# Another fixed order for chunks 0 to 5 of a chunked recurrence and for the weight conversion beside it, and a ring of five tiles

## The chip, the cores and the metric

One Trainium2 chip, one core. The metric is the device time of one execution in microseconds (us), the median of three runs.

## What is computed

A recurrence over 768 steps for 4 x 8 heads of 40 x 40 state, and two layers on its output. Cut to the core of the reference:

```python
for t in range(S):                       # S = 768, B = 4, H = 8, D = 40
    y[:, :, t] = einsum('bhd,bhde->bhe', r_t, state)
    Sa = einsum('bhde,bhe->bhd', state, a_t)
    state = state * w_t - einsum('bhd,bhe->bhde', Sa, b_t) + einsum('bhd,bhe->bhde', v_t, k_t)
x = y as 3072 rows of 320
g = elu(x @ w_in); x = g @ w_out         # first MoE: 320 -> 2048 -> 320
P = exp(x @ w_gate - max), 8 rounds of row and column scaling
out = sum over 8 experts of P[:, e] * (relu(x @ w1[e]) @ w2[e])   # 320 -> 1024 -> 320
```

The weights of the first MoE come as 64-bit floats, read as pairs of 32-bit words.

## The kernel before

**The recurrence** is cut into 24 chunks of 32 steps. For a chunk, products over all pairs of its steps are made with matmuls, a triangular system is solved, and the state goes on to the next chunk. The work of a chunk is split into functions, named by what they do:

- `loadw`, `loadk`, `loadv`, `loads2` (tokens `ldw`, `ldk`, `lu`, `lv`) issue the loads of the chunk's inputs on SyncE's DMA queue: tiles `WA`, `KE`, `VU`, `rB` and `rO`.
- `prep` (lines 331 to 355) has five steps: the scan of decays into `F` on VectorE, reciprocal and second scan into `xE`, a product `aE`, copies on ScalarE, and two products that write `KE` in place (line 355, on VectorE in chunks 0 and 1, on GpSimd later).
- `E3` (masked products, line 383, evicted by VectorE into `Am`) writes the chunk's matrix to DRAM (`Ad`, line 400); `LT` reads it back, spread over the partitions (line 408). `E1` transposes `KE` into `KB`, `E2` (line 369) transposes `xE` into `xT`.
- `tsolve` (token `u` with two chunks, then `s_n` for n steps) solves the systems of two chunks together on VectorE, two short instructions a step (lines 436 and 438, tiles `Tt` and `Wk`). The result goes to DRAM and back on SyncE's queue (`Td`, line 460, `TT`, line 464).
- `H1` to `H4` carry the state: `H1` makes the right-hand side `RH`, `H2` multiplies by the solved matrix (line 510) and corrects the second half of the chunk (lines 500 and 501), `H3` makes the new state `Y` (line 534), `YW` scales it on GpSimd (line 486). `O1`, `O2`, `O3a`, `O3b` make the output: `O1` copies into `uE` on ScalarE and VectorE, `O2` a masked product `Gm`, `O3b` multiplies by `xT` and writes the rows to DRAM (`yd`).

**The conversion** of the first MoE's weights is 32 pieces, 16 of `w_in` (384 wide) and 16 of `w_out` (320 wide). Token `d` loads a piece into `raw` (two buffers for each size), `b` puts the words together in three VectorE instructions (lines 214 to 216, tile `tmp`), `o` rounds and takes the remainder on ScalarE and GpSimd into `Wt` and `Wo` (lines 238 to 245).

**The first MoE** runs beside the recurrence in units of 128 hidden columns (token `m`): eight matmuls into `ph` (line 638), the activation on ScalarE and VectorE (`m`, `g`, line 647; `gh`, `gl`, line 651 on GpSimd), and, two units later, eight matmuls into two accumulators (lines 665 to 669). Token `x` transposes the next block of rows. A unit can only run when its weights are converted.

**The order** of all this is written by hand, as tokens. The table `START` covers chunks 0 to 3 whole, the early steps of chunks 4 to 7 and the whole conversion. After it a loop over chunks runs the table `order2` for chunks 4 and 5 and `order` for the rest; `+3` in a token is a chunk ahead, `p` three steps of a running solve. The instructions of TensorE, VectorE, ScalarE and GpSimd are pinned to that order, queue by queue. SyncE's queue is not: a scheduler places its DMAs.

```python
for t in tokens(PLAN["start"]):
    ...
    pin_since(last, late_queue=PLAN["queue"])   # "queue": False
```

After the last chunk the rest of the first MoE and the second MoE follow, with TensorE busy throughout.

Of the kernel before, what the change touches and what calls it, by code (L numbers as in the profile page):

```python
# [9 lines left out]
F32 = mybir.dt.float32  # L10
# [10 lines left out]


START = """
lu_0 prep_0*5 E3_0 ldw_2 E3_0 LT_0 E1_0 E2_0 prep_1*5 E3_1*2 LT_1 ldk_2 E4_0 H1_0 E1_1 E2_1 lu_1 d*2 lv_0 b o u_0_1 d b o prep_2 d prep_2*2 ldw_3 b
s_10 s_11 b prep_2 s_10 o d prep_2 E3_2 b o E3_2 LT_2 E2_2 ldk_3 H2_0 o E1_2 prep_3*2 d*2 H2_0 prep_3 H2_0 O1_0 H3_0 prep_3*2 E3_3 b H3_0 o O1_0 d
E3_3 YW_1 ldw_4 b E4_1 LT_3 O2_0 H1_1 E1_3 prep_4 ldk_4 E2_3 u_2_3 b o d O2_0 s_10 O3b_0 d lu_2 o H2_1 O3a_0 O3b_0 s_10 H2_1 s_10 prep_4 H2_1 prep_4
ldw_5 H3_1*2 b o d O1_1*2 H4_1 lv_1 YW_2 O2_1 E4_2 prep_4*2 E3_4 b O3a_1 d O2_1 o prep_5 H1_2 O3b_1 b E3_4 LT_4 o O3b_1 s_9 E1_4 ldk_5 xl E2_4 d
prep_5 H2_2 prep_5 x*2 b x*2 H2_2 prep_5 m prep_5 o ldw_6 b o d m H2_2 d E3_5 b m E2_5 E3_5 H3_2*2 E1_5 ldk_6 o d O1_2 prep_6*2 lu_3 m O1_2 H4_2 YW_3
E4_3 m b o d u_4_5 prep_6 H1_3 lv_2 b O2_2 ldw_7 m o O2_2 d LT_5 H2_3 b o d s_10 m H2_3 O3a_2 b o d m O3b_2*2 H2_3 prep_6*2 b prep_7 ldw_8 d o H3_3 m
E3_6 H3_3 b o d m E3_6 E2_6 E1_6 ldk_7 m b d o LT_6 s_10 prep_7 O1_3 H4_3 lu_4 b YW_4 m d o O1_3 b o lv_3 O2_3 b o d m O2_3 prep_7 b o d m O3a_3 b  # L30
O3b_3 s_20 d b o m d m prep_7 b m o prep_7 m*2 O3b_3 d m o d m x b o b d m x b d o*2 x*2 b o
"""


# [5 lines left out]
    "start": START,  # L40
    "tp": ((3, 3), (3, 3)),
    "queue": False,
# [71 lines left out]
def build(ctx, tc, r, k, v, w, a, b, w_in, w_out, wg, w1, w2, wa_d, kb_d, re_d, ro_d, vt_d, wp_d, consts, out, C, off):  # L114
# [13 lines left out]
    V, A, G, T, SY = nc.vector, nc.scalar, nc.gpsimd, nc.tensor, nc.sync  # L128
# [49 lines left out]
    r2 = rec.enter_context(tc.tile_pool(name="r2", bufs=2, side="right"))  # L178
# [178 lines left out]
    def unpad(dst, ps):  # L357
        return dst.rearrange("p (j g e) -> p j g e", j=2, g=NG), ps.rearrange("p (g x) -> p g x", g=NG)[:, :, 0:128].rearrange("p g (j x) -> p j g x", j=2)[:, :, :, 0:D]
# [9 lines left out]

    def E2(c):
        z = st[c]  # L370
        z.xT = r2.tile([128, 384], F32, tag="xT", name="xT", bufs=4)
        xv = z.xC
        for g in range(NG):
            T.transpose(PS["E2"][0][:, 128 * g:128 * g + HR], xv[0:HR, g, :], ident[0:HR, 0:HR])
        o, i = unpad(z.xT[:, 0:DM], PS["E2"][0])
        cp("XT", 0, o, i)
# [91 lines left out]
    def cp(n, i, out, in_):  # L468
        (A.copy if PLAN["eng"][n][i] == "A" else G.tensor_copy if PLAN["eng"][n][i] == "G" else V.tensor_copy)(out=out, in_=in_)
# [661 lines left out]
    with ExitStack():  # L1131
# [37 lines left out]
        mg = msteps()  # L1169
        wgen = [(k, i) for i in range(NF1) for k in "io"]  # L1170
        fns = dict(ld=loads, ldw=loadw, ldk=loadk, lu=loadv, lv=loads2, prep=prep, H1=H1, H2=H2, H3=H3, H4=H4, E1=E1, E2=E2, E3=E3, E4=E4, T=tsolve, O1=O1, O2=O2, O3a=O3a, O3b=O3b, YW=YW, LT=LT)
        done = {("ld", 0), ("ld", 1)}

# [140 lines left out]
```

## Time and profile before

| | us |
|---|---|
| median of three runs | 2249.49 |
| lowest and highest run | 2245.49 and 2250.47 |
| the profiled execution | 2250.63 |
| its span, first to last instruction | 2248.8 |

The profile shows for every engine (PE is TensorE, DVE VectorE, ACT ScalarE, POOL GpSimd, SP SyncE) when it was busy, and what ended its idle time. A line of the timeline has the start, the duration and, in brackets, the idle time in front and its releaser. The granted clock is that of TensorE: 1.00 is its level of 2.4 GHz, 0.50 that of 1.2 GHz.

### The profile page before, as it was taken

Reading aid. Unit: us, or ns where it says so; the run is one execution under the profiler, and the core shown is the slowest. Engines: PE = TensorE matmul, PEld = TensorE weight load, DVE = VectorE, ACT = ScalarE, POOL = GpSimd, SP = SyncE. Lnnn points to the kernel's source line nnn. Section 1 sums busy time; section 2 is a strip of 40 time slices with the busy share of each in tenths; the row PEclk is TensorE's granted clock in tenths of the full one; section 3 lists DMA queues with packets and bytes.
Section 4 is the critical chain, followed back from the end, with each engine's and each line's share of the span. In section 5 each row is a group of like instructions: output and inputs, shape, how many; then the busy total and the mean of one; then the engine's idle time right before and its main releaser. Section 6 shows DMA issues by size and latency. Waiting matters only on the chain.

```text
span 2248.8 us, 48229 instructions
## 1 busy us (share of the span) xinstructions
PE 2137.9 (95%) x20483; PEld 1934.8 (86%) x20483; DVE 928.5 (41%) x1889; ACT 815.0 (36%) x1813; POOL 439.7 (20%) x545
## 2 busy tenths in 40 slices
PE   3788999999999999999999999999999999999998
PEld 2677888999898989898888888888888888888888
DVE  6686667777766322532222222222222222222222
ACT  2344555555544565223224324223224212112111
POOL 2354333443433261002002002002002002001000
PEclk9676999999999999999999999999999999999999
DMA  6654434344442142002113112002002001000000
GB/s 161 165 161 107 114 102 100 95 110 111 105 105 72 45 122 56 29 1 56 20 20 75 23 32 78 26 27 78 27 26 65 1 1 52 1 1 20 24 24 25
DMA packets 216657, 138.50 MB, mean 62 GB/s; under 512 B 143793, under 2 KB 192306, under 8 KB 216434
## 3 DMA queue, kind: packets, MB, share of 16 engines
q1 hardware_dynamic: 216434, 135.34, 22.9%
q8 instruction: 162, 2.65, 0.5%
q14 instruction: 61, 0.50, 0.1%
HBM read 116.80 MB, written 18.48 MB: 60 GB/s over the span
## 4 chain that ended last, share of the span: by engine, by line
PE 79%; DVE 9%; DMA 4%; issue 2%; ACT 2%; SPq 2%; POOL 1%; DVEq 0%; ACTq 0%; POOLq 0%
PE h L874 28%; PE pa L918 10%; PE pa L919 10%; PE pa L917 10%; PE ph L638 5%; PE h L863 2%; PE a L665 2%; DVE Wk L452 2%; DVE Tt L445 2%; DMA yd<-xT 1%; PE P L534 1%; PE a L666 1%; PE a L667 1%; PE P L383 1%; PE P L510 1%
## 5 line engine op out<-in xcount | busy, mean ns | idle before, releaser
L878 DVE SCALAR_TENSOR_TENSOR hl<-h,hh 128x512 fp32r<-128x512 f32 x384 | 265.3, 691 | 765.9 <-ACT hh L877 765.4
L877 ACT ACTIVATE hh<-h 128x512 fp32r<-128x512 f32 x384 | 229.6, 598 | 899.2 <-PE h L874 897.5
L874 PE MATMUL h<-xs,a 128*128 128x512 f32 x2280 | 547.0, 394 | 0.2 <-DVE hl L878 0.2
L874 PEld LDWEIGHTS h<-xs,a 128*128 128x128 f32 x2280 | 421.0, 188 | 109.8 <-issue 25.4
L918 PE MATMUL pa<-a,hl 128*128 128x320 f32 x1536 | 475.8, 310 | 0.8 <-DVE hl L878 0.8
L919 PE MATMUL pa<-a,hh 128*128 128x320 f32 x1536 | 475.2, 309 | 0.0
L917 PE MATMUL pa<-a,hh 128*128 128x320 f32 x1536 | 473.9, 309 | 0.3 <-ACT logits L692 0.3
L918 PEld LDWEIGHTS pa<-a,hl 128*128 128x128 f32 x1536 | 288.9, 188 | 6.7 <-DVE hl L878 1.7
L917 PEld LDWEIGHTS pa<-a,hh 128*128 128x128 f32 x1536 | 288.6, 188 | 5.2 <-ACT logits L692 0.4
L919 PEld LDWEIGHTS pa<-a,hh 128*128 128x128 f32 x1536 | 289.0, 188 | 0.0
L825 POOL TENSOR_TENSOR a<-rw,a 128x384 fp32r<-128x384 f32 x64 | 65.2, 1019 | 1057.5 <-ACT a L823 1044.4
L638 PE MATMUL ph<-X,Wt 128*128 128x256 f32 x1536 | 234.8, 299 | 8.2 <-DVE g L647 7.8
L651 POOL TENSOR_TENSOR gl<-g,gh 128x256 fp32r<-128x256 f32 x192 | 150.1, 782 | 385.1 <-ACT gh L649 305.0
L638 PEld LDWEIGHTS ph<-X,Wt 128*128 128x128 f32 x1536 | 212.2, 205 | 13.1 <-DVE g L647 11.5
L647 DVE SCALAR_TENSOR_TENSOR g<-m,ph 128x256 f32<-128x256 f32 x192 | 79.9, 416 | 205.0 <-ACT m L641 147.9
L928 DVE SCALAR_TENSOR_TENSOR acc<-pa,Pg,acc 128x320 f32<-128x320 f32 x168 | 81.0, 544 | 184.1 <-PE pa L919 184.1
L649 ACT ACTIVATE gh<-g 128x256 fp32r<-128x256 f32 x192 | 80.1, 417 | 163.5 <-DVE g L647 162.7
L452 DVE TENSOR_TENSOR Wk<-Wk,Tt 128x132 f32<-128x132 f32 (+24 forms) x279 | 109.4, 392 | 8.6
L874 PE MATMUL h<-X,a 128*128 128x512 f32 x456 | 108.9, 394 | 0.0
L640 ACT ACTIVATE m<-ph 128x256 f32<-128x256 f32 x192 | 73.0, 380 | 89.5 <-PE ph L638 86.4
L874 PEld LDWEIGHTS h<-X,a 128*128 128x128 f32 x456 | 84.1, 188 | 21.9 <-issue 5.0
L445 DVE TENSOR_TENSOR Tt<-Wk,LT 128x132 f32<-128x132 f32 (+24 forms) x279 | 90.1, 323 | 8.0
(189 smaller groups left out, 2700.3 us busy)
## 6 DMA issues: line engine op xcount, KB each, us to landing
LT<-Ad SPq DMA_DIRECT2D x22, 512.0 KB
rw<-in_moe_w SPq DMA_DIRECT2D x64, 160.0 KB
WA<-in_wa SPq DMA_DIRECT2D x23, 422.9 KB
KE<-in_kb SPq DMA_DIRECT2D x23, 416.0 KB
rw<-in_moe_w SPq DMA_DIRECT2D x64, 128.0 KB
VU<-in_vt SPq DMA_DIRECT2D x24, 320.0 KB
raw<-in_wp SPq DMA_DIRECT2D x16, 384.0 KB
rchk<-in_wp SPq DMA_DIRECT2D x16, 384.0 KB
```

What stands on the lines that cost most here:

```text
L445: V.tensor_tensor(out=tv, in0=Wk[:, :, 0:ni, j:j + 1].to_broadcast(sh), in1=LT2[:, :, j, j + 1:C].unsqueeze(2).to_broadcast(sh), op=ALU.mult,)
L452: V.tensor_tensor(out=Wk[:, :, 0:ni, j + 1:C], in0=Wk[:, :, 0:ni, j + 1:C], in1=tv, op=ALU.subtract)
L638: T.matmul(ph, lhsT=Wt[0:kp, wi, 128 * f:128 * f + 128], rhs=X[0:kp, xi, :], start=(i == 0), stop=(i == 7))
L649: A.activation(out=gh, in_=g, func=AF.Copy)
L651: G.tensor_tensor(out=gl, in0=g, in1=gh.bitcast(F32), op=ALU.subtract)
L874: T.matmul(h, lhsT=a1[:, wi, :], rhs=X[bk][:, xi, :], start=(i == 0 and n == 8), stop=(i == n - 1), skip_group_check=(n == 7))
L877: dve["hh"] = A.activation(out=hh, in_=h, func=AF.Relu)
L878: V.scalar_tensor_tensor(out=hl, in0=h, scalar=0.0, in1=hh.bitcast(F32), op0=ALU.max, op1=ALU.subtract)
L917: T.matmul(o, lhsT=hh[:, ts_], rhs=a2[:, 0, :], start=(f == 0), stop=False)
L918: T.matmul(o, lhsT=hl[:, ts_], rhs=a2[:, 0, :], start=False, stop=False)
L919: T.matmul(o, lhsT=hh[:, ts_], rhs=a2[:, 1, :], start=False, stop=(f == NF2 - 1))
L928: V.scalar_tensor_tensor(out=at, in0=o, scalar=Pg[:, tt, e:e + 1], in1=at, op0=ALU.mult, op1=ALU.add)
```

## The change

It replaces the table `START` and the table `order2` by others with the same tokens (300 and 68 of them, each as often as before), and gives `xT` five tiles where it had four. The number of instructions on each engine stays. Two lines of the tables as an example, and the one line of code outside them:

```diff
-lu_0 prep_0*5 E3_0 ldw_2 E3_0 LT_0 E1_0 E2_0 prep_1*5 E3_1*2 LT_1 ldk_2 E4_0 H1_0 E1_1 E2_1 lu_1 d*2 lv_0 b o u_0_1 d b o prep_2 d prep_2*2 ldw_3 b
+prep_0*3 lu_0 prep_0*2 E3_0 ldw_2 E3_0 E2_0 prep_1*5 E3_1*2 LT_1 ldk_2 E1_1 E2_1 E4_0 H1_0 lu_1 d*2 lv_0 b o E1_0 u_0_1 d b o prep_2 d prep_2 LT_0
...
-        z.xT = r2.tile([128, 384], F32, tag="xT", name="xT", bufs=4)
+        z.xT = r2.tile([128, 384], F32, tag="xT", name="xT", bufs=5)
```

In `order2` the tokens `O3a`, `m`, `G`, `YW`, `O2` and one `E3` stand elsewhere.

**VectorE, the solve of chunks 0 and 1.** `Tt` and `Wk` are the solve's own tiles, `tmp` is a converted piece.

```order
 L436 TENSOR_TENSOR Tt<-Wk,LT 128x60
-L214 TENSOR_SCALAR tmp<-raw 128x320
-L215 SCALAR_TENSOR_TENSOR tmp<-raw,tmp 128x320
-L216 SCALAR_TENSOR_TENSOR tmp<-raw,tmp 128x320
 L438 TENSOR_TENSOR Wk<-Wk,Tt 128x4x3x5
...
 L436 TENSOR_TENSOR Tt<-Wk,LT 128x16
 L438 TENSOR_TENSOR Wk<-Wk,Tt 128x4x4
+L214 TENSOR_SCALAR tmp<-raw 128x320
+L215 SCALAR_TENSOR_TENSOR tmp<-raw,tmp 128x320
+L216 SCALAR_TENSOR_TENSOR tmp<-raw,tmp 128x320
 L214 TENSOR_SCALAR tmp<-raw 128x384
```

A piece of `w_out` (320 wide) that stood between two steps of the solve now stands behind its last step.

**SyncE's queue in the first microseconds.** `Ad` is the matrix of a chunk on its way to DRAM, `LT` the way back, `KE` the input of chunk 2, `raw` a piece to be converted.

```order
 L1242 DMA wgs<-in_moe_w_gate 64x8 x2
 L400 DMA Ad<-Am_114 32x8x32 x4
-L315 DMA KE<-in_kb 104x1024
 L327 DMA rO<-in_ro 104x512
...
 L226 DMA raw<-in_moe_w_out 128x640
-L226 DMA raw<-in_wp 128x768
-L310 DMA WA<-in_wa 104x1041
-L226 DMA raw<-in_moe_w_out 128x640
+L315 DMA KE<-in_kb 104x1024
+L226 DMA raw<-in_wp 128x768
+L310 DMA WA<-in_wa 104x1041
```

The load of `KE` for chunk 2 was behind the writes of chunk 0's matrix, ahead of both `LT` reads; it now stands behind both and behind a `raw` load. (`ldk_2` kept its place in the table; the buffer it writes is read by `E1_0`, which comes later now.)

**VectorE before the end of the solve of chunks 4 and 5.** `g` is a unit of the first MoE, `uE` the copy of `O1_3`, `F` the first scan of chunk 7.

```order
 L438 TENSOR_TENSOR Wk<-Wk,Tt 128x4x3x6
+L647 SCALAR_TENSOR_TENSOR g<-m,ph 128x256
 L336 SCALAR_TENSOR_TENSOR F<-WA,dr 104x528
 L214 TENSOR_SCALAR tmp<-raw 128x320
 L215 SCALAR_TENSOR_TENSOR tmp<-raw,tmp 128x320
 L216 SCALAR_TENSOR_TENSOR tmp<-raw,tmp 128x320
-L647 SCALAR_TENSOR_TENSOR g<-m,ph 128x256
-L469 COPY uE<-P_102 80x512
 L214 TENSOR_SCALAR tmp<-raw 128x384
 L215 SCALAR_TENSOR_TENSOR tmp<-raw,tmp 128x384
 L216 SCALAR_TENSOR_TENSOR tmp<-raw,tmp 128x384
+L469 COPY uE<-P_102 80x512
```

`g` goes ahead of the scan and of a piece, and `uE` goes behind the next piece.

## Rows read from the trace of the kernel before

**Rows 1.** The head of the page, and its row of the granted TensorE clock, 40 slices
```profile
span 2248.8 us, 48229 instructions
...
PEclk9676999999999999999999999999999999999999
```

**Rows 2.** Busy time by stretch: us, busy us of each engine, granted clock, DMA share, GB/s
```profile
core 0: us, PE busy (x) PEld busy (x) DVE busy (x) ACT busy (x) POOL busy (x), PEclk, DMA share, GB/s
...
111.00:177.00 66.00, 56.96 (x955) 51.92 (x955) 57.84 (x106) 29.46 (x71) 36.87 (x48) 0.71 0.57 163
177.00:198.00 21.00, 12.20 (x144) 11.00 (x144) 11.87 (x23) 8.56 (x22) 11.58 (x18) 0.75 0.49 126
198.00:218.00 20.00, 19.47 (x272) 18.07 (x272) 9.16 (x14) 8.85 (x22) 5.82 (x8) 0.50 0.25 68
218.00:258.00 40.00, 38.83 (x755) 36.69 (x754) 35.65 (x84) 22.08 (x56) 13.31 (x17) 1.00 0.37 96
...
900.00:2249.00 1349.00, 1341.86 (x7512) 1185.93 (x7510) 370.01 (x644) 368.81 (x706) 99.40 (x106) 1.00 0.11 30
```

**Rows 3.** TensorE's waits from 30 to 130 us: total, times, longest
```profile
PE P L510 <- DMA TT<-Td: 11.9, 2, 11.3
```

**Rows 4.** TensorE's waits from 130 to 210 us
```profile
PE P L383 <- DVE uE L469: 3.7, 1, 3.7
PE P L510 <- ACT RH L469: 3.6, 1, 3.6
PE ph L638 <- DVE g L647: 3.4, 2, 2.4
PE a L666 <- POOL gl L651: 3.1, 1, 3.1
```

**Rows 5.** Pieces of the chain that ended last: start, us, what
```profile
26.48 2.45 DMA Ad<-Am
29.08 3.69 DMA LT<-Ad
...
68.56 3.61 DMA Ad<-Am
...
178.22 1.95 DMA Td<-Wk
```

**Rows 6.** VectorE in order of time, around the first solve
```profile
32.86 0.22 DVE L436 TENSOR_TENSOR Tt<-Wk,LT 128x60 f32<-128x60 f32 x1 [0.45 <-DMA LT<-Ad]
...
40.84 0.32 DVE L214 TENSOR_SCALAR tmp<-raw 128x320 int32<-128x320 int32 x1
...
42.13 0.21 DVE L438 TENSOR_TENSOR Wk<-Wk,Tt 128x60 f32<-128x60 f32 x1
```

**Rows 7.** VectorE in order of time, around the second solve
```profile
76.11 0.22 DVE L436 TENSOR_TENSOR Tt<-Wk,two 128x60 f32<-128x60 f32 x1 [5.08 <-DMA two<-Ad]
...
84.30 1.25 DVE L336 TENSOR_TENSOR_SCAN F<-WA,dr 104x528 f32<-104x528 f32 x1
...
87.73 0.49 DVE L542 TENSOR_TENSOR Y<-P,Yw 104x320 f32<-104x320 f32 x1 [0.21 <-PE P L534]
88.14 0.46 DVE L214 TENSOR_SCALAR tmp<-raw 128x384 int32<-128x384 int32 x1
```

**Rows 8.** VectorE in order of time, around the third solve
```profile
163.69 0.33 DVE L214 TENSOR_SCALAR tmp<-raw 128x320 int32<-128x320 int32 x1 [0.63 <-POOL WoB L245]
...
170.59 0.41 DVE L647 SCALAR_TENSOR_TENSOR g<-m,ph 128x256 f32<-128x256 f32 x1
...
187.07 0.90 DVE L214 TENSOR_SCALAR tmp<-raw 128x384 int32<-128x384 int32 x1 [3.85 <-DMA raw<-in_wp]
```

**Rows 9.** The DMA queue of SyncE, the load of chunk 2
```profile
21.55 0.33 SPq L315 DMA_DIRECT2D KE<-in_kb  x1
```

**Rows 10.** TensorE, the same eight products at either clock
```profile
199.94 2.07 PE L638 MATMUL ph<-X,Wt 128*128 128x256 f32 x8
...
219.97 1.19 PE L638 MATMUL ph<-X,Wt 128*128 128x256 f32 x8
```

More of the change, by code (lines that the diff above doesn't have):

```diff
@@ L23 @@
 START = """
-lu_0 prep_0*5 E3_0 ldw_2 E3_0 LT_0 E1_0 E2_0 prep_1*5 E3_1*2 LT_1 ldk_2 E4_0 H1_0 E1_1 E2_1 lu_1 d*2 lv_0 b o u_0_1 d b o prep_2 d prep_2*2 ldw_3 b
-s_10 s_11 b prep_2 s_10 o d prep_2 E3_2 b o E3_2 LT_2 E2_2 ldk_3 H2_0 o E1_2 prep_3*2 d*2 H2_0 prep_3 H2_0 O1_0 H3_0 prep_3*2 E3_3 b H3_0 o O1_0 d
-E3_3 YW_1 ldw_4 b E4_1 LT_3 O2_0 H1_1 E1_3 prep_4 ldk_4 E2_3 u_2_3 b o d O2_0 s_10 O3b_0 d lu_2 o H2_1 O3a_0 O3b_0 s_10 H2_1 s_10 prep_4 H2_1 prep_4
+prep_0*3 lu_0 prep_0*2 E3_0 ldw_2 E3_0 E2_0 prep_1*5 E3_1*2 LT_1 ldk_2 E1_1 E2_1 E4_0 H1_0 lu_1 d*2 lv_0 b o E1_0 u_0_1 d b o prep_2 d prep_2 LT_0
+prep_2 ldw_3 b d prep_2 s_11 s_10*2 o b prep_2 E3_2 b o E3_2 o LT_2 E2_2 ldk_3 H2_0 E1_2 prep_3*2 d*2 prep_3 H2_0*2 O1_0*2 H3_0 prep_3*2 E3_3 b H3_0 o
+d E3_3 YW_1 ldw_4 b E4_1 LT_3 O2_0 H1_1 prep_4 E1_3 prep_4 ldk_4 E2_3 u_2_3 b o d O2_0 s_10 lu_2 o H2_1 d O3a_0 O3b_0*2 s_10 H2_1 s_10 H2_1 prep_4
 ldw_5 H3_1*2 b o d O1_1*2 H4_1 lv_1 YW_2 O2_1 E4_2 prep_4*2 E3_4 b O3a_1 d O2_1 o prep_5 H1_2 O3b_1 b E3_4 LT_4 o O3b_1 s_9 E1_4 ldk_5 xl E2_4 d
[L28 to L31, printed above, removed]
+prep_5 H2_2 x prep_5 x*2 b x H2_2 prep_5 m prep_5 o ldw_6 b o d H2_2 d E3_5 E2_5 m E3_5 b m H3_2*2 E1_5 ldk_6 o d O1_2 prep_6*2 lu_3 m O1_2 H4_2 YW_3
+E4_3 m b o d lv_2 b u_4_5 prep_6 H1_3 O2_2 ldw_7 m o O2_2 d LT_5 H2_3 b o m H2_3 O3a_2 b o d*2 s_10 m O3b_2*2 H2_3 prep_6 b prep_7 ldw_8 prep_6 d m
+H3_3 E3_6 H3_3 b o*2 d m E3_6 E2_6 E1_6 ldk_7 m b d o LT_6 s_10 H4_3 lu_4 m prep_7 O1_3 b YW_4 b o lv_3 d o O1_3 O2_3 b o d m O2_3 b o d prep_7 b
+O3b_3 s_20 m O3a_3 d b o m d m o m prep_7 b prep_7 m*2 d m o d m x O3b_3 b o b d x b d o m o x*2 b o
 """
```

2 rows, old and new, of the table PLAN are left out of this document.

## The prediction

> **What bounds the kernel now.** I read the head of the page first. The granted clock is below one only in the first slices and 0.9 behind them [rows 1], so the kernel falls into an uneven beginning and a long even rest. The table by stretches says the same: from 900 us on TensorE is busy in 1341.86 of 1349 us at the full clock, and from 218 to 258 in 38.83 of 40 [rows 2]. Work that is only put in another order cannot shorten those. Every piece that the tables hold is done before or shortly behind 258 us, and what follows starts when they end; so the question is by how much the beginning ends earlier.
>
> There, three things take turns. Up to the first solve everything waits for data: TensorE stands 11.9 us in all, in two waits, for the solved matrices to come back from DRAM [rows 3], and the way there is a chain of DMAs and of VectorE [rows 5, 6]. From 111 to 177 us it is VectorE, busy in 57.84 of 66 us [rows 2]: the conversion, the solve of chunks 4 and 5 and the units share it. From 177 to 198 TensorE is busy in 12.20 of 21 us, and the waits in front of that end with ScalarE's `RH` (3.6 us), which stands in ScalarE's queue behind the last converted pieces; these came late because a piece's load had been queued behind the solve's own DMAs (VectorE idle 3.85 us for it) [rows 2, 4, 8].
>
> **The change part by part.**
>
> *A converted piece leaves the first solve.* Its three instructions begin at 40.84 us, the solve goes on at 42.13 [rows 6]: 1.29 us between two dependent steps, on the path, since TensorE waits for that solve [rows 3]. The piece now follows the solve, where VectorE next waits for TensorE. Gain 1.3 us.
>
> *The load of `KE` for chunk 2 goes behind both `LT` reads.* It was issued at 21.55 us, ahead of them [rows 9]. The last write of chunk 1's matrix took 2.45 us to land with that load in flight; a `Td` write of the same size took 1.95 us at 178.22 [rows 5]. So 0.5 us for chunk 1, and as much again if chunk 0's writes were held as well: between 0 and 1.0 us. I take 0.5, from the row that is this very write. There is no more in it: the solve starts 0.45 us after VectorE is free [rows 6]. The product on GpSimd that needs `KE` gets it later, but its reader on TensorE then still waits for the solve, long after. The Trainium skill, "DMA: Bandwidth & Descriptors", section "Queues, rings and completion order", says that an engine takes the descriptors of a ring in order; by that, the load, issued behind chunk 0's writes, never held them, and the gain is the 0.5 us of chunk 1 alone, where writes that share the load's fate would give 1.0. No row here shows the single packets.
>
> *One piece more between the first and the second solve.* The extra piece, and the first scan of chunk 4 (1.25 us at 84.30, behind the second solve before, ahead of it now), fall into VectorE's wait of 5.08 us for `LT` of chunk 3 [rows 7]: cost 0. The scan's leaving gains nothing either, for behind the second solve the next step is `Y`, which waits for TensorE (until 87.73), and the piece behind it at 88.14 opens the way to chunk 4's products [rows 7]. What can cost is DMA: the next `raw` load is released later and lands beside the writes of chunk 3's matrix. These already took 3.61 us against 2.45 for chunk 1's [rows 5]; one more such step is 1.2 us. Between 0 and 1.2 I take 0, since the loads around them only change places.
>
> *The long stretch of VectorE.* Before the end of the third solve there stand the same pieces, scans and copies as before, less one `g` (0.41 us), which falls to the far side, into the wait of 3.85 us: 0.4 us. `uE` now fills the 0.63 us in which VectorE waited for GpSimd's part of a piece at 163.69 [rows 8]: 0.6 us. Together 1.0, bounds 0 (both covered by other waits) and 1.0.
>
> *What TensorE pays for the late `uE`.* TensorE waited 3.7 us for `uE` [rows 4], and now waits for a piece's three instructions more, 1.3 us [rows 6], and at the next unit it waits for a `g` that comes behind the end of the third solve instead of at 170.59 [rows 8]. Behind these stand waits of 3.4, 3.1 and 3.6 us in the same window [rows 4], which end with VectorE, GpSimd and ScalarE, not with TensorE: 0 as long as they are there. The unit moved ahead of `H3_3` likewise fills a wait of TensorE's and shifts `Y` by less than a microsecond: 0.
>
> *Behind the third solve* the DMAs stand in the same order and the pieces too; the path from the solve over the queue, the 3.85 us and the last piece to `RH` keeps its length. *`order2`* moves work inside a stretch in which TensorE is busy in 38.83 of 40 us [rows 2]: 0. *The fifth tile* lets `xT` be written without waiting for the output of four chunks ago; no wait for that output is among TensorE's waits here [rows 4]: 0.
>
> Sum: 1.3 + 0.5 + 1.0 = 2.8 us. The profiled execution took 2250.6, so 2247.8 in its own terms. It lay 1.1 us above the median of the runs shown, 2249.5; against that, **2246.7 us**. With the bounds: at best 1.3 + 1.0 + 1.0 = 3.3, 2246.2; at worst 1.3 - 1.2 = 0.1, 2249.4. About 0.2% (4.5 us) is what a measurement of this kernel can tell from no change, so this is within it.
>
> **The rivals.**
>
> *The clock comes up earlier: faster.* From 198 to 218 us TensorE is busy in 19.47 of 20 us, and the granted clock is 0.50, the level of 1.2 GHz; from 218 it is 1.00 [rows 2]. Before 198 it had been idle for much of 21 us. The same eight products take 2.07 us at 199.94 and 1.19 at 219.97 [rows 10], 1.74 times as long. At the full clock the stretch would take 19.47 / 1.74 = 11.2 us, 8.3 less; half of that with the 2.8 gives 7.0, **2242.5 us**, all of it 2238.4. For it: TensorE's waits between 157 and 198 are dealt out anew. Against: the 3.6 us ahead of 198 stay. The Trainium skill, "TensorE: Matmul & The Clock Gate", section "What's actually happening", says that sustained activity releases the half rate; by that rule the stretch at 198 should have been fast soon after it began, and the time would come out near the lower figure. The row of this trace does not agree: 20 us nearly without a gap, at 0.50.
>
> *The clock comes up later: slower.* The other side of the same: if the half rate lasts beyond 218, each microsecond of full-clock work in the stretch behind costs 0.74 more. From 9.9 us on (7.3 / 0.74) this outweighs the gain by over 4.5 us and decides; with 12 us it is 8.9 - 2.8 = 6.1 more than now, **2255.6 us**. For it: the late `uE` and `g` add to TensorE's waits between 157 and 180. Against: the first product behind them waits for the same chain.
>
> *The gain is lost on the way: no change.* What the first solve gains, `Ad` of chunk 3 gives back (the 1.2 us above), and VectorE's waits for TensorE in the long stretch take the rest: **2249.4 us**. For it: `Y` and `X` there wait for others.
>
> **How the numbers follow.** Forecast 0.46, earlier clock 0.31, later clock 0.15, lost 0.08. Faster by over 0.2% (below 2245.0) are the earlier clock and 0.03 of the forecast: 0.34. Slower (above 2254.0) is the later clock: 0.15. The rest is 0.51. The range goes from 2239.0, which holds nearly all of the earlier clock, to 2255.0, which cuts the later clock in its middle. Since cases of both signs are in it: the forecast's own range is 2245.0 to 2249.5.
>
> **What would show it.** Right, step by step: no `tmp` instructions inside the first solve, and the second solve's first step at about 74.3 us where it stood at 76.11; the wait for `raw` ending at 184.3 where it ended at 187.07 [rows 7, 8]; TensorE's wait for `uE` above 3.7 us with nothing late behind 198. A second solve that starts at 76 means that the DMA bounds took it. If the stretch at 1.2 GHz behind the last piece ends at another distance than 20 us, the clock decided, and the forecast is wrong whatever the steps did.

## The result: 1.3% faster, and the profile after

| | us | |
|---|---|---|
| kernel before, 6 runs | 2249.98 | 2245.49 to 2254.44 |
| changed kernel, 6 runs | 2221.74 | 2213.65 to 2225.39 |
| ratio | 0.9872 | 95% interval 0.9851 to 0.9894 |
| forecast | 2246.7 | range 2239.0 to 2255.0 |

The kernel is 28 us faster, and the forecast was wrong. Of the two profiled executions the spans are 2248.8 and 2223.5 us. The head of the changed kernel's page, with its row of the granted clock:

```profile
span 2223.5 us, 48220 instructions
...
PEclk9686999999999999999999999999999999999999
```

Beside [rows 1] this row says nothing: at 56 us a slice both kernels look even from the fifth slice on, since a 9 stands for 0.90 or more. To see where the time went I took the moment at which the eviction of a chunk's new state `Y` begins in either trace:

| state of chunk | before | after | earlier by |
|---|---|---|---|
| 1 | 87.04 | 85.53 | 1.5 |
| 5 | 244.06 | 239.24 | 4.8 |
| 8 | 339.92 | 330.18 | 9.7 |
| 12 | 461.31 | 450.09 | 11.2 |
| 16 | 585.91 | 568.20 | 17.7 |
| 20 | 711.20 | 683.37 | 27.8 |
| 22 | 766.31 | 738.40 | 27.9 |

Up to chunk 5, which is as far as the new tables reach, 4.8 us are won. The other 23 come between chunk 5 and chunk 20, in a loop whose table the change does not touch. The one thing of the change that acts there is the ring of `xT`. (Behind chunk 22 the changed kernel loses 2.6 of the 27.9 again: the two spans differ by 25.3.) The stretches of equal work, by the table of stretches (columns as in [rows 2]), first of the kernel before:

```profile
244.50:804.50 560.00, 532.27 (x9346) 506.91 (x9344) 359.11 (x852) 295.65 (x757) 204.37 (x254) 0.96 0.37 94
```

and of the changed kernel:

```profile
240.00:777.00 537.00, 519.99 (x9346) 496.98 (x9345) 357.01 (x851) 294.77 (x758) 205.46 (x254) 0.98 0.39 98
```

The same 9346 matmuls take 23 us less. TensorE's idle time falls from 27.7 to 17.0 us, and its busy time from 532.3 to 520.0, at a granted clock of 0.98 instead of 0.96. So in this pair of profiles nearly half of the gain (10.7 us) is waiting that is gone, and the other half (12.3) are matmuls that take less time. Summed over stretches of 2 us, the half clock holds for 41 us of the first stretch and for 20 of the second; at the ratio of 1.74 of [rows 10] the 20 us of difference make some 9 of the 12.3 (an estimate), and where the other 3 come from is not shown.

Who waited is seen on ScalarE. Its waits from 258 to 860 us (waiting tile and line, releaser: total, times, longest) in the kernel before, with TensorE's longest in the same time as the last row:

```profile
ACT gh L649 <- DVE g L647: 135.3, 117, 2.7
ACT m L640 <- PE ph L638: 69.2, 54, 3.1
ACT xT L469 <- DMA yd<-xT: 32.4, 8, 5.3
ACT RH L469 <- PE P L481: 17.8, 15, 1.8
...
PE P L365 <- ACT xT L469: 13.3, 6, 2.9
```

and on ScalarE in the changed kernel, where the third row is gone (TensorE's row is gone too):

```profile
ACT gh L649 <- DVE g L647: 136.0, 121, 3.2
ACT m L640 <- PE ph L638: 78.4, 57, 6.4
ACT RH L469 <- PE P L481: 17.8, 14, 1.8
```

**One such wait in full.** In the round of chunk 18 the table runs `O3b` for chunk 17, which writes its rows from `xT` to DRAM, and soon after `E2` for chunk 21. With four tiles that is the same tile. The timeline of the kernel before, GpSimd's copy that completes the rows, and SyncE's queue:

```profile
629.09 0.24 POOL L599 COPY xT<-xT 128x64 f32<-128x64 f32 x1 [1.33 <-PE P L481]
```

```profile
630.06 2.36 SPq L464 DMA_DIRECT2D TT<-Td  x4
632.47 1.17 SPq L460 DMA_DIRECT2D Td<-Wk  x2
633.68 0.61 SPq L408 DMA_DIRECT2D LT<-Ad  x1
634.40 0.54 SPq L603 DMA_DIRECT2D yd<-xT  x1
635.04 2.03 SPq L464 DMA_DIRECT2D TT<-Td  x4
```

The rows are ready at 629.33, but their write is issued at 634.40, behind the solve's transfers; by the chain of waits, which goes on from it to ScalarE's `VU`, it takes 5.05 us to land:

```profile
634.40 5.05 DMA yd<-xT
```

In the rounds between, the same write on the same queue lands sooner. SyncE's read of the rows, `yt`, waits for the landing (it follows at 639.46 here), and there it comes 1.9 to 3.3 us behind the write, as in

```profile
601.55 0.35 SPq L603 DMA_DIRECT2D yd<-xT  x1
604.21 0.34 SPq L615 DMA_DIRECT2D yt<-yd  x1
```

ScalarE and TensorE in the round of chunk 18:

```profile
639.55 0.43 ACT L469 COPY xT<-P 128x320 f32<-128x320 f32 x1 [5.32 <-DMA yd<-xT]
640.00 1.77 ACT L516 ACTIVATE VU<-P 32x320 f32<-32x320 f32 x4
```

```profile
640.02 0.93 PE L365 MATMUL P<-cst,KE 104*128 104x104 f32 x8 [2.94 <-ACT xT L469]
640.89 0.27 PE L534 MATMUL P<-VU,KB 64*40 64x40 f32 x4
641.37 1.99 PE L534 MATMUL P<-VU,KB 64*40 64x40 f32 x60 [0.21 <-ACT VU L516]
```

Nobody is in haste for `xT` itself. But the copy stands in ScalarE's queue ahead of `VU`, which the new state needs, and until it is done it holds the PSUM bank (where TensorE's products go) into which `E1` must write next. So TensorE waits 2.94 us. What the clock then does, in stretches of the kernel before:

```profile
637.00:640.00 3.00, 0.08 (x1) 0.00 (x0) 0.00 (x0) 0.43 (x2) 0.00 (x0) 1.00 0.76 182
640.00:643.00 3.00, 2.77 (x68) 2.52 (x70) 0.00 (x0) 2.86 (x8) 0.71 (x2) 0.71 0.72 187
643.00:646.00 3.00, 3.00 (x24) 2.92 (x21) 1.85 (x3) 1.04 (x4) 2.04 (x4) 0.50 0.32 108
646.00:649.00 3.00, 3.00 (x20) 3.00 (x19) 0.96 (x3) 1.60 (x4) 0.72 (x2) 0.65 0.37 99
649.00:652.00 3.00, 3.00 (x44) 2.86 (x43) 2.88 (x5) 2.60 (x6) 3.00 (x3) 1.00 0.54 140
```

TensorE is idle from 637 to 640, and behind that the granted clock is at 0.50 for some 7 us, although TensorE works nearly without a gap. In the changed kernel the same round has `xT` copied at 616.95, before the write of chunk 17's rows is even issued (617.40), and the clock stays at 1.00:

```profile
616.95 0.41 ACT L469 COPY xT<-P 128x320 f32<-128x320 f32 x1
618.15 1.77 ACT L516 ACTIVATE VU<-P 32x320 f32<-32x320 f32 x4 [0.79 <-PE P L510]
```

```profile
618.00:621.00 3.00, 3.00 (x34) 2.83 (x32) 0.73 (x1) 2.71 (x7) 0.56 (x1) 1.00 0.93 271
621.00:624.00 3.00, 3.00 (x80) 2.95 (x78) 1.84 (x3) 1.20 (x4) 2.04 (x4) 1.00 0.61 153
```

### The profile page after: what moved, and what is told of

Same layout as the page of the kernel before. It is cut to its first block, busy times and chain, and to the rows that moved or that the text cites. A ratio compares the mean times of both kernels' runs of the same rounds, so it can differ in the third digit from the quotient of the medians.

```text
span 2223.5 us, 48220 instructions
## 1 busy us (share of the span) xinstructions
PE 2118.7 (95%) x20483; PEld 1918.0 (86%) x20483; DVE 922.6 (41%) x1889; ACT 814.6 (37%) x1813; POOL 443.6 (20%) x545
## 4 chain that ended last, share of the span: by engine, by line
PE 78%; DVE 9%; DMA 4%; issue 3%; ACT 2%; SPq 2%; POOL 1%; DVEq 0%; ACTq 0%; POOLq 0%
PE h L874 29%; PE pa L918 10%; PE pa L917 10%; PE pa L919 10%; PE ph L638 5%; PE h L863 3%; DVE Wk L452 2%; DVE Tt L445 2%; PE a L665 1%; PE P L383 1%; PE P L510 1%; PE a L666 1%; PE a L667 1%; PE P L534 1%; DVE g L647 1%
## 5 line engine op out<-in xcount | busy, mean ns | idle before, releaser
L638 PE MATMUL ph<-X,Wt 128*128 128x256 f32 x1536 | 228.4, 293 | 5.1 <-DVE g L647 5.1
L638 PEld LDWEIGHTS ph<-X,Wt 128*128 128x128 f32 x1536 | 206.2, 199 | 8.3 <-DVE g L647 7.2
```

Source lines behind the costliest of these rows:

```text
L638: T.matmul(ph, lhsT=Wt[0:kp, wi, 128 * f:128 * f + 128], rhs=X[0:kp, xi, :], start=(i == 0), stop=(i == 7))
```

## The experiments

All ratios are to the kernel before, run on the same chip in the same job.

| run | edit | ratio | 95% interval |
|---|---|---|---|
| `e1_ring5_only` | five tiles, old order | 0.9884 | 0.9866 to 0.9902 |
| `e2_order_only` | new order, four tiles | 0.9999 | 0.9986 to 1.0012 |
| `e4_ring6` | the change with six tiles | 0.9879 | 0.9859 to 0.9899 |
| `e5_late_E2` | old order, four tiles, `E2` later | 0.9966 | 0.9952 to 0.9980 |
| `e6_later_E2` | the same, two units later still | 0.9906 | 0.9890 to 0.9922 |
| `e7_yd_other_queue` | old order, four tiles, GpSimd issues the write | 0.9885 | 0.9868 to 0.9902 |
| `e8_earlier_E2` | old order, four tiles, `E2` earlier | 1.0049 | 1.0031 to 1.0067 |
| `e9_piece_out_of_solve` | old order less one place, four tiles | 0.9994 | 0.9981 to 1.0007 |
| `e10_after_other_queue` | the change, GpSimd issues the write | 0.9871 | 0.9849 to 0.9893 |

**The ring alone, the order alone.** The first is the kernel before with this edit, the second the changed kernel with it undone:

```diff
-        z.xT = r2.tile([128, 384], F32, tag="xT", name="xT", bufs=4)
+        z.xT = r2.tile([128, 384], F32, tag="xT", name="xT", bufs=5)
```

> The kernel before with five tiles of xT and nothing else. Theory R (the ring): in the kernel before ScalarE's copy into xT waits 32.4 us in eight times for the row write of four chunks ago, and from the step of chunk 5 to that of chunk 22 the changed kernel is 23.5 us shorter; so this kernel takes 2249.98 - 23 = 2227, between 2223 and 2231, and ScalarE's wait for yd is gone. Rival O (the order of chunks 0 to 5 sets how the later chunks fall): 2246 or more, and the wait is small while the steps of the later chunks keep about 61 us for two.

> The changed kernel with the ring back at four tiles. Theory R: only the early gain stays, 4.4 us at the step of chunk 5, so 2245.6, between 2242 and 2250, with ScalarE waiting some 30 us for yd again. Rival O: 2221 to 2228, as the changed kernel.

The ring alone gives 0.9884 (2220.09 against 2245.29 us, 25.2 less), the whole change 0.9872: the intervals overlap. The order alone gives 0.9999. Theory R holds for the ring (2 us more than it said) and rival O is out. What theory R left to the order, the early gain of 4.4 us, does not show in the time: the interval goes from 3.1 us faster to 2.7 us slower. In the run with the order alone ScalarE's wait is back, from 258 to 860 us:

```profile
ACT xT L469 <- DMA yd<-xT: 36.0, 8, 5.6
```

**A sixth tile** (`bufs=6`).

> The changed kernel with six tiles of xT. Theory R: no wait of ScalarE for yd is left with five, so a sixth gives nothing: 2221.7, between 2218 and 2226. A rival, that the wait moved on and still holds something: below 2217.

0.9879, as with five; its median of 2216.85 us is under the 2217 that I named for the rival, but on a chip on which the kernel before took 2245.29 and not 2249.98, and the ratio decides. Five tiles were enough.

**Must it be a tile?** The same wait can be attacked without one, by putting `E2` later in `order`:

```diff
-... m xl p m E2+3 p p p p lv G prep+4 H2 m m E1+3 ldk+4 prep+4 H3 m m x prep+4 ...
+... m xl p m p p p p lv G prep+4 H2 m m E1+3 ldk+4 prep+4 H3 E2+3 m m x prep+4 ...
```

> The kernel before with four tiles, but in the order of the later chunks the transposition into xT stands behind the first part of the new state (after E1, the next chunk's steps and one part of H3) instead of ahead of H2. Theory R in its narrow form (what counts is the time from the row write to the next copy into the same tile, since the state's own copy stands behind the waiting one in ScalarE's queue): the wait of 4 to 5 us is covered, 2227 to 2235. Rival (the tile itself is needed, the wait only moves to the new place and holds the outputs there): 2245 or more.

0.9966: neither theory as I put it. The wait for the row write is gone, but TensorE's waits from 218 to 860 us now begin with another:

```profile
PE P L374 <- ACT KB L469: 16.5, 8, 2.7
```

`E2` stands close behind `E1` here, with only a part of `H3` between them, and both use one PSUM bank; `E2` waits until ScalarE has copied `E1`'s result into `KB`. One wait had made room for the next. So `E2` went two units further back (`H3 m m E2+3 x prep+4`):

> The kernel before with four tiles; the transposition into xT stands two units of the first MoE further back than in the run with the late transposition, where the wait for the row write was gone but TensorE waited 16.5 us in eight times for ScalarE's copies into KB (both use one PSUM bank) and the gain was a third of the ring's. Theory R in its narrow form (only the time between the write of a row tile and the next copy into it counts, a fifth tile is one way to have it): both waits gone, 0.988 to 0.992 of the kernel before, 2218 to 2228. Rival (the tile itself is needed: with four, something else waits wherever the transposition stands): 0.995 or more.

0.9906, that is 2225.15 against 2248.82 us. TensorE's wait for `KB` is 2.4 us (218 to 860, as above), ScalarE waits for no row write, and most of the gain is there with four tiles. So the tile itself is not needed; the time between a tile's write and its next use is what this edit and the fifth tile have in common.

**The queue or the traffic.** Here the row write is issued from another queue, in the kernel before:

```diff
-            SY.dma_start(out=yd[c], in_=y)
+            G.dma_start(out=yd[c], in_=y)
```

> The kernel before with four tiles, in which GpSimd issues the row write itself, right behind its own copy, instead of SyncE. Theory Q (the queue: at chunk 15's round the row is ready at 629.33, and its write is issued at 634.40, behind the solve's own six writes and four reads on SyncE's queue): the write starts 5 us earlier, lands before or shortly behind the moment when ScalarE comes to the copy (634.2), and most of the 32.4 us of waiting goes: 0.988 to 0.993, 2218 to 2230, if an issue on GpSimd costs little. Rival T (the traffic: the write needs 5 us because it lands beside a 512 KB read, and will be as late wherever it is issued): 0.997 or more with ScalarE still waiting over 20 us.

(The round named there is that of chunk 18, not 15.) 0.9885: theory Q. In the timeline of this run GpSimd issues the write right behind its copy:

```profile
583.20 0.33 POOL L599 COPY xT<-xT 128x64 f32<-128x64 f32 x1
583.93 0.59 POOL L603 DMA_DIRECT2D yd<-xT  x1 [0.41 <-POOL xT L599]
```

and by the view of the tile the writes land in 2.6 us in the median:

```profile
DMA to landing us min/median/max: 2.2/2.6/4.9
```

ScalarE waits for the write once, for 0.2 us. So the wait was made of two things: a place behind the solve's transfers in SyncE's queue, and a landing that took 3.8 to 5.05 us in the seven rounds in which it stood in the chain of waits of the kernel before. Rival T is out: issued right behind GpSimd's copy, the write lands sooner, not as late. As far as the runs tell, the shorter landing belongs to the moment and not to the queue, since SyncE's writes took 1.9 to 3.3 us in the rounds between.

**The wait made longer.** `E2` two units earlier (`m m p p E2+3 m xl p m p p p p`):

> The kernel before with four tiles and the transposition into xT two units of the first MoE earlier, which makes the suspected wait longer: 2 to 4 us more in each of the eight rounds that waited, and some 2 us in each of the eight others (their write is issued at 601.55 and landed by 605.9, the copy would come at some 603). Theory R: ScalarE's wait goes from 32 to between 55 and 90 us, and at the price seen so far (25 us of time for 32.4 us of waiting) the time rises by 15 to 45 us: 1.007 to 1.020. Rival (ScalarE is busy for only 53 of 100 us there, its wait has slack and the fifth tile helps in another way): within 4 us of the kernel before.

The time rises, as theory R says, but by less than it said: 1.0049, some 11 us. ScalarE's wait from 258 to 860 us rose to 53.0 us, under the 55 to 90 expected:

```profile
ACT xT L469 <- DMA yd<-xT: 53.0, 13, 7.3
```

The price failed too: 20.6 us more of this wait cost 11, where taking 32.4 away had brought 25. The trace shows why it is smaller: TensorE's own wait for `xT` stays (14.2 us against 13.3, 258 to 860); what is new is 7.3 us of waiting for `VU` (1.0 before):

```profile
PE P L365 <- ACT xT L469: 14.2, 7, 3.0
PE P L534 <- ACT VU L516: 7.3, 13, 0.6
```

**The piece in the first solve alone.** The old table with one `b` moved:

```diff
-s_10 s_11 b prep_2 s_10 o d prep_2 ...
+s_10 s_11 prep_2 s_10 b o d prep_2 ...
```

> The kernel before with one edit: the converted piece inside the first solve goes behind its last step. Theory: the solve takes 11.7 us before and 9.8 to 10.0 in the three traces with the changed table, so it ends 1.3 to 1.9 us earlier here too, and the time by no more than that: 2243.5 of 2245.3, which a measurement does not tell from none (0.998 to 1.001). Rival (this piece carries all of the 2.6 us by which the state of chunk 4 comes earlier in the mean of three traces of each table): state of chunk 4 at 210.3 rather than 212.9.

The solve runs from 32.85 to the start of its last step at 42.94, 10.1 us, where before it took 11.7; the time cannot be told from unchanged (0.9994). The state of chunk 4 comes at 216.41, later than in the kernel before (214.36), which speaks against the rival; but it is one trace, and traces of one table differ by up to 4.9 us there (below), so it does not settle it.

**Both remedies together.**

> The changed kernel (five tiles, new order) with the row write issued by GpSimd. Both remedies treat the same wait, so together they should give what one gives: 0.986 to 0.989 of the kernel before, as the fifth tile alone (0.988) and the other queue alone (0.9885). Rival: the row write also holds the solve's own transfers behind it on SyncE's queue, and off that queue it frees them: 0.984 or less, 2212 or less.

0.9871: nothing on top. None of these runs is faster than the changed kernel by more than the intervals.

## Why the prediction was wrong, by its own steps

*The step that failed* is "The fifth tile lets `xT` be written without waiting for the output of four chunks ago; no wait for that output is among TensorE's waits here [rows 4]: 0." It should have been 25 us: the run with the ring alone gives that. Three readings were at fault. [Rows 4] is TensorE's list from 130 to 210 us, and the waits come in every second chunk from 269 to 702. The wait is not TensorE's but ScalarE's, whose list I never took; TensorE's share of it appears there under another releaser, ScalarE's copy. And ahead of it stands "the kernel falls into an uneven beginning and a long even rest", for which [rows 2] show 218 to 258 and then 900 on: nothing between, where the recurrence runs. There TensorE was idle for 27.7 of 560 us, at a granted clock of 0.96 that [rows 1] show as a 9 (0.90 or more), and the chain that ended last goes through seven landings of row writes, 32.0 us together. The page has them in its fourth part, the chain's shares by line:

```profile
PE h L874 28%; PE pa L918 10%; PE pa L919 10%; PE pa L917 10%; PE ph L638 5%; PE h L863 2%; PE a L665 2%; DVE Wk L452 2%; DVE Tt L445 2%; DMA yd<-xT 1%; PE P L534 1%; PE a L666 1%; PE a L667 1%; PE P L383 1%; PE P L510 1%
```

A tile whose ring the change enlarges is named in that line. The name alone does not settle it: the chain of the changed kernel still goes through four such landings, but there SyncE's read of `yt` follows, and not a copy of ScalarE's:

```profile
381.59 4.26 DMA yd<-xT
...
385.86 0.34 SPq L615
```

With ScalarE's waits beside it, the wait could have been seen in the profile of the kernel before; what it was worth could not. The rows there give 32.4 us on ScalarE and 13.3 on TensorE, and the run with the ring gives 25.

*The order: 2.8 us, within what can be told.* That it cannot be told from none held: the order alone is 0.9999, with an interval of -3.1 to +2.7 us. The 2.8 us themselves are not shown; they lie at the edge of that interval. The single steps, in the trace of the changed kernel:

```profile
42.59 0.19 DVE L438 TENSOR_TENSOR Wk<-Wk,Tt 128x16 f32<-128x16 f32 x1
42.70 0.33 DVE L214 TENSOR_SCALAR tmp<-raw 128x320 int32<-128x320 int32 x1
...
74.44 0.22 DVE L436 TENSOR_TENSOR Tt<-Wk,two 128x60 f32<-128x60 f32 x1 [3.26 <-DMA two<-Ad]
...
182.69 0.36 DVE L214 TENSOR_SCALAR tmp<-raw 128x384 int32<-128x384 int32 x1 [2.88 <-DMA raw<-in_wp]
188.45 0.36 DVE L214 TENSOR_SCALAR tmp<-raw 128x384 int32<-128x384 int32 x1 [2.49 <-DMA raw<-in_wp]
```

- *The piece out of the first solve, 1.3 us*: the solve's first to last step went from 11.70 us (32.86 [rows 6] to 44.56) to 10.04 (32.55 to 42.59), 1.7 us; the piece now follows at 42.70, and no `tmp` instruction is left inside. Right, and 0.4 us more than said.
- *The load of `KE`, 0.5 us*: the first solve begins at 32.55 where it began at 32.86 [rows 6]. But the six traces with the old tables in this study begin it between 32.09 and 33.39 (mean 32.6), the four with the new ones between 32.43 and 32.66 (32.6). No gain that can be seen; it lies at the lower bound. The 0.5 us rested on the load being under way when the write of 2.45 us was issued at 26.48 [rows 5], 4.9 us behind the load's own issue [rows 9], and no row shows that. GpSimd's product with `KE` comes later, as the forecast said, and its reader on TensorE with it (40.89 us, where it stood at 37.14 behind a wait of 11.6 that [rows 3] do not list); but TensorE still waits for the solved matrix behind it, until 49.48, so the lateness costs nothing.
- *The second solve at about 74.3*: it begins at 74.44, against 76.11 [rows 7]. Right, and the scan and the extra piece did find cover, as [rows 7] said; the four traces with the new tables have 74.06 to 74.71, the six with the old ones 74.75 to 77.10.
- *The wait for `raw` ending at 184.3*: it ended at 182.69, against 187.07 [rows 8], 1.6 us earlier than said; but a second wait of 2.49 us followed, where the kernel before had two of 1.35 and 0.50 (at 192.55 and 195.17).
- *TensorE's late `uE`, with "nothing late behind 198"*: the wait rose from 3.7 to 5.3 us and that for `RH` from 3.6 to 5.2 [rows 4]. The last piece came 5 us earlier all the same (190.24 instead of 195.17).

The waits of TensorE from 130 to 210 us in the changed kernel:

```profile
PE P L383 <- DVE uE L469: 5.3, 1, 5.3
PE P L510 <- ACT RH L469: 5.2, 1, 5.2
```

For the early part as a whole, the state of chunk 4 comes at 210.6 us in the mean of the four traces with the new tables (209.29 to 211.71) and at 213.2 in that of the six with the old ones (211.15 to 216.04). That is 2.7 us (213.22 less 210.56) and near the forecast, but the old tables alone spread over 4.9 us, and the measured times resolve nothing. Whether these 2.7 us are there, and which step gives them, stays open. In the pair of profiles what is won up to that state is not the waiting that the forecast counted: TensorE is busy for 143.3 us of 214.36 before and 137.4 of 209.29 after, so it is idle for 71.0 and 71.9.

*The rivals of the clock*, as the prediction put them, are out. The stretch at half the clock behind the last piece moved with that piece: in the kernel before the piece begins at 195.17 and the clock is back at 218, 22.8 us later, in the changed kernel at 190.24 and 213, 22.8 us later:

```profile
212.00:213.00 1.00, 1.00 (x7) 0.91 (x5) 1.00 (x2) 0.99 (x3) 0.92 (x1) 0.50 0.61 217
213.00:214.00 1.00, 1.00 (x10) 1.00 (x9) 1.00 (x3) 0.98 (x2) 0.00 (x0) 0.90 0.60 162
```

Ahead of that stretch the clock did differ (mean granted clock 0.75 up to the state of chunk 4 before, 0.79 after), and whether the change did that is not shown. Where it mattered to the time is the loop of the later chunks, where the forecast did not look: some 9 of the 23 us won there are, by the estimate above, matmuls that no longer run at 1.2 GHz behind a stall.

## What to carry to other kernels

Where a change enlarges a ring, find in the trace who waits for the transfer that frees its tiles, over the whole time in which the ring turns and on every engine that writes into it; a list of the bottleneck's own waits in one stretch does not show it, while the chain that ended last names it, and what follows the transfer there tells whether it is the ring that waits. A copy that nobody needs soon can still be dear if it waits in an in-order queue ahead of one that is needed now. And before buying another buffer, look why the transfer is late: here moving its issue to a free queue, or the next use some microseconds back, was worth nearly as much.

## What the runs showed of the hardware

A wait of TensorE of 2.94 us was followed by some 7 us at a granted clock of 0.50 (1.7, 3.0 and 2.1 us of the three stretches from 640 to 649, by their means), with TensorE busy nearly throughout. At the ratio of 1.74 of [rows 10] these lose 2.9 us (an estimate), as much as the wait itself. Two of ScalarE's eight waits for the row write did not stop TensorE: behind the one that ended at 454.33 there is no slow stretch, and the slow stretch at 269 follows another wait, of 1.58 us for `TT`. Of the six that did stop it, five (1.87 to 2.94 us) are followed by one; the sixth, of 1.62 us, which ended at 579.41, is not, and why is not shown.

The same holds from trace to trace. Over the equal work from chunk 5 to 38 us behind the state of chunk 22, the half clock, summed over stretches of 2 us, holds for 34 to 48 us in the four traces in which ScalarE waits for the row write (among them before 41, order only 34, longer wait 48), for 27 in `e5_late_E2`, where the wait for `KB` took its place, and for 7 to 20 in the other six, in which the wait is gone (among them ring only 10, changed kernel 20).

The same row write of 192 KB landed in 2.6 us in the median (2.2 to 4.9) when GpSimd issued it behind its own copy. On SyncE's queue it took 3.8 to 5.05 us among the solve's transfers, where the kernel before had it in its chain of waits, and 1.9 to 3.3 us in the rounds between. By the view of the tile an issue held GpSimd for 0.58 us in the median.
